# The second half's factors made row-wise and transposed by the DMA on load: a two-branch kernel on one core

## The chip, the core and the metric

The kernel runs on one core of a Trainium2 chip. The metric is device time in microseconds, as the median of several executions. Five engines work side by side, each on its own queue of instructions in order: PE (TensorE, matrix products), DVE (VectorE), ACT (ScalarE), POOL (GpSimd) and SP (SyncE, which issues most transfers here). Sixteen DMA engines move the data; the profile gives their mean busy share. SBUF is the on-chip memory with 128 partitions, PSUM the memory into which PE writes, DRAM the large memory outside.

## What is computed

```
xn = layernorm(A_q)                                   # 2048 x 1024
conv(kv): kv = shiftconv(A_k) * A_v; y = longconv(kv, A_ssm_k) + kv * A_ssm_D
out = A_q + xn * y + silu(xn @ B_w1) @ B_w2            # B_w1 1024 x 3584, B_w2 3584 x 1024
```

The first branch is a causal convolution of length 2048 for each of 1024 channels. The second is a feed-forward block with 3584 hidden units. All inputs are 32-bit floats. Large products are made with 16-bit parts: each operand is split into a high and a low half-precision part, and three products (high x high, high x low, low x high) are added.

## The kernel before, in words

**The row tiles.** The 2048 rows are 16 tiles of 128 rows by 1024 columns. `load_row` loads each into a buffer `xt`, `ln_rows` normalizes it in place (line 501). PE needs the 1024 columns on partitions, so `transposes` (line 507) turns each 128 x 128 block on PE by a product with an identity (line 520), four blocks to one PSUM bank `ft`.

**The products.** The first large product is made by Strassen's scheme: each 2 x 2 block product takes seven products P1 to P7 in place of eight, with sums of blocks as operands. The operands on the side of x are A11, A12, A22, S1, S2, S3, S4 (`PRODUCTS`, line 39): with the upper tile's halves A11, A12 and the lower tile's halves A21, A22, S1 = A21 + A22, S2 = S1 - A11, S3 = A11 - A21, S4 = A12 - S2. Tiles 0 to 3 (upper) and 4 to 7 (lower) make the operands of the first half, tiles 8 to 11 and 12 to 15 those of the second. One operand of one half is a tile of 128 partitions by 4 row tiles by 4 column blocks by 2 parts by 128, 16-bit: 1024 KB, one of eight places `x0` to `x7` (`XPLACE`, line 41).

`units` (line 948) runs 12 units of the first half, then 14 of the second. A unit's products run in the order P7, P6, P2, P5, then P1 of the next unit, P3, P4; each is 12 matrix instructions 512 wide, lines 912 to 914 in turn, so four of line 912 mark one product. Weight factors stand in a pool `wo`. For units 0 and 1 of the second half they were kept there; those of units 2 to 13 are loaded back (`load_factors`, line 783, `wo<-ws`).

**The second half's operands.** The place of an operand comes free when the last unit of the first half has read it. So the second half's operands are made early, from about 125 to 200 us, and stored in DRAM. `lower_sums` (line 570) and `upper_sums` (line 585) take the transposed blocks from PSUM, make the sums in buffers of the rings `s`, `s1` and `xst`, and hand each operand to `spill` (line 643). That splits it into its two 16-bit parts (`split`, line 352: ACT writes the high part, line 342; DVE the low part, line 334; DVE's sums are line 331) and stores it in `xsp`. `load_x` (line 985) later loads each operand with one plain transfer of 1024 KB, as soon as its place is free and all 28 stores have landed.

**What sets the order.** The order is planned when the program is built. Each piece of work is an `Op` with an engine, a busy time and, for a transfer, its bytes. `Order.run` (line 165) takes, again and again, the stream whose next piece can start first by the model, less a bias that acts as a priority (0.02 for the spill work here, 0.06 for `load_x`). `L` (line 322) is the cost of a plain load or store issued by SP. What comes out is a fixed order for each engine and for SP's queue of transfers; at run time every instruction waits in that order for its semaphores.

The convolution starts when the operands of the second half are stored (`change`, line 1695); from then on its work on DVE and ACT, and its smaller products on PE (lines 1437, 1471 to 1473, 1664 to 1666), are woven between the units. Its loads, the stores of the hidden values (`hs`, `hsf`), and copies of x to the output (`out<-in_x`, line 1185) stand in the same SP queue.

`Ring` is a set of equal buffers, `Halves` a set of larger buffers that are given out whole or by halves. `quad` (line 795) makes the same four sums for the second large product, in place and with rows on partitions.

Of the kernel before, what the change touches and what calls it, by code (L numbers as in the profile page):

```python
# [13 lines left out]
F16 = mybir.dt.float16  # L14
# [4 lines left out]
ADD, SUB, MUL = ALU.add, ALU.subtract, ALU.mult  # L19

P = 128
# [6 lines left out]
KH = KD // 2  # L28
NF = F // P
NP = NF // 2  # L30
W = 512
# [4 lines left out]
XS = 512.0  # L36
# [69 lines left out]
class Order:  # L106
# [182 lines left out]
def h3_ffn_kernel(ctx, tc, x, kp, vs, fs, shift, dskip, w1, w2, cfwd, cinv, out):  # L289
    nc = tc.nc  # L290
    ctx.enter_context(tc.manual_schedule())
    order = Order()
    add = order.add
    flag = defaultdict(Token)
# [12 lines left out]
    def size(a):  # L307
        n = 1
        for s in a.shape[1:]:
            n *= s  # L310
        return n
# [10 lines left out]
    def L(o, i, m=0.3):  # L322
        n = size(o) * o.shape[0] * mybir.dt.size(o.dtype)
        return Op("SP", 0.4, 0.1, lambda: nc.sync.dma_start(o, i), [i], [o], m, n)

    def G(o, i, m=0.3):
        n = size(i) * i.shape[0] * mybir.dt.size(i.dtype)
        return Op("POOL", 1.1, 3.0, lambda: nc.gpsimd.dma_start(o, i, accum_op=ADD), [i], [o], m, n)  # L328

    def v_tt(o, a, b, op, **k):  # L330
        return V(lambda: nc.vector.tensor_tensor(o, a, b, op=op), o, [a, b], **k)  # L331
# [32 lines left out]
    xsp = {p[0]: dram.tile([P, 4, KH, 2, P], F16, name=f"xsp{p[0]}") for p in PRODUCTS.values()}  # L364
# [38 lines left out]
    lnp = early.enter_context(tc.tile_pool(name="lnp", bufs=1))  # L403
# [1 line left out]
    ft = Ring(order, ps_e, "ft", 3)  # L405
    nm = Ring(order, ps_e, "nm", 1)
    xts_r = Ring(order, lnp, "xt", 12)
    sums_r = Ring(order, lnp, "s", 4)
    s1_r = Ring(order, lnp, "s1", 4)
    xst_r = Ring(order, lnp, "xst", 3)  # L410
    raw_r = Ring(order, rawa, "raw", 4)
    t1_r = Ring(order, rawa, "t1", 1)
    sq_r = Ring(order, rawa, "ss", 2)
# [93 lines left out]
    def transposes():  # L507
        jobs = [(t, a) for t in range(4) for a in range(2)]
        jobs += [(4 + i, a) for i in range(4) for a in range(2)]
        for i in range(4):  # L510
            jobs += [(12 + i, 0), (12 + i, 1), (8 + i, 0), (8 + i, 1)]
        for t, a in jobs:
            yield flag["xn", t]
            xn, tok = xns[t]
            yield ft.ready
            pt, ptok = ft.tile([P, KH, P], uses=2)

            def mm():
                for c in range(KH):
                    nc.tensor.transpose(pt[:, c, :], xn[:, (KH * a + c) * P:(KH * a + c + 1) * P], ident)  # L520
            yield T(mm, pt, [xn], 0.5, m=0.3)
            tok.set()
            pts.append((pt, ptok))
# [34 lines left out]
    def next_transposed():  # L558
        yield next_pt
        return pts.pop(0)  # L560
# [9 lines left out]
    def lower_sums(to, ring):  # L570

        a21, k21 = yield from next_transposed()
        c21, kc = yield from next_sum(sums_r, 1)
        yield a_act(c21, a21, AF.Copy)
        k21.set()
        give(to, "A21", a21, k21)
        a22, k22 = yield from next_transposed()
        s1, ks1 = yield from next_sum(ring, 2)
        yield v_tt(s1, a22, c21, ADD)
        k22.set()  # L580
        give(to, "A22", a22, k22)
        give(to, "S1", s1, ks1)
        return c21, kc, s1, ks1

    def upper_sums(to, ring, c21, kc, s1, ks1, t=None):

        if t is not None:
            yield flag["kept", t]
        a11, k11 = kept[t][0] if t is not None else (yield from next_transposed())
# [8 lines left out]
        a12, k12 = kept[t][1] if t is not None else (yield from next_transposed())  # L598
# [9 lines left out]
    def x_rows():  # L608
        yield from first_rows()
        second["A21"], second["tok"] = places[4].tile([P, 4, KH, 2, P], F16)  # L610
        for name in ("A22", "S2", "S3", "S1", "S4"):
            r = places[XPLACE[name]]
            yield r.ready
            xo[0][name], xtok[0][name] = r.tile([P, 4, KH, 2, P], F16)

        class Kept:
            bias = 0.14

            def __init__(self, i):
# [17 lines left out]
        class Spilled(Kept):  # L637
            bias = 0.02

            def __call__(self, name):  # L640
                return None if name == "A21" else lambda src, tok: spill(xsp[name][:, self.i], src, tok)

        def spill(o, src, tok):
            yield lambda: s1_r.ready() or xst_r.ready()
            r = s1_r if s1_r.ready() else xst_r
            st, stok = r.tile([P, KH, 2, P], F16)
            yield from split(st[:, :, 0], st[:, :, 1], src, XS, (tok,))
            yield L(o, st)
            stok.set()
            flag["spilled"].set()  # L650

        yield 0.02
        for i in range(4):
            part = yield from lower_sums(Spilled(i), sums_r)
            yield from upper_sums(Spilled(i), sums_r, *part)
        flag["x done"].set()

    for name in ("A11", "A12", "A21", "A22", "S1", "S2", "S3", "S4"):
        flag["x", 0, name] = Token(4)
# [325 lines left out]
    def load_x():  # L985
        yield flag["spilled"]
        for name in [p[0] for p in PRODUCTS.values()]:
            r = places[XPLACE[name]]
            yield r.ready
            xo[1][name], xtok[1][name] = r.tile([P, 4, KH, 2, P], F16)  # L990
            yield L(xo[1][name], xsp[name])
            flag["x", 1, name].set()


# [802 lines left out]
```

## Time and profile before

| | |
|---|---|
| median of 3 executions | 1277.92 us (1276.17 to 1280.69) |
| the profiled execution | 1277.71 us |
| its span on the core | 1275.9 us |
| mean granted TensorE clock | 0.994 |
| DMA, all queues | 284.55 MB, mean 223 GB/s |
| issues of `x<-xsp` | 7 of 1024 KB |
| issues of `xsp<-s` and `xsp<-xst` | 28 of 256 KB |

The span is the stretch of time that the profile shows, from the first to the last instruction. A row of a group gives line, engine, operation, output and inputs by name, the shapes, the count, then busy time and mean duration, then the engine's idle time ahead of the group with what ended it. A row of the order of time begins with start and duration in microseconds. Rows by stage give the stretch, its length and each engine's busy time in it. A row of transfers gives name, queue, count, size and the median time from issue to landing. PE instructions overlap in a pipeline: one of 512 columns is shown as 0.38 us long, but the next starts 0.21 or 0.22 us after it.

### The profile page before, as it was taken

The numbers are of one execution on the slowest core, as the hardware profiler recorded it, in microseconds if no ns is written. First come the engines' busy times: TensorE is split into PE (matmuls) and PEld (weight loads), VectorE is DVE, ScalarE is ACT, GpSimd is POOL, SyncE is SP. The second block draws the span as 40 slices with busy tenths as digits, with TensorE's granted clock in tenths as the row PEclk, the third lists the DMA queues.
The fourth block names the chain that finished last, engine by engine and source line by source line (L and its number), as shares of the span: only waits on it lengthen the run. The fifth ranks groups of instructions, "written<-read, shape, count | busy, mean of one in ns | idle before, by whom it ended". The sixth has DMA issues, their size and how long they took to land.

```text
span 1275.9 us, 17270 instructions
## 1 busy us (share of the span) xinstructions
PE 1244.9 (98%) x6146; PEld 609.6 (48%) x6146; DVE 1148.4 (90%) x1533; ACT 729.5 (57%) x1169; POOL 132.9 (10%) x141
## 2 busy tenths in 40 slices
PE   7899999999999999999999999999999999999997
PEld 6444444444444544445444544544444454454453
DVE  8999997998899879999899799899979989998981
ACT  6867887878776777559651722653452263544231
POOL 0000000000000110002100300300020030123132
PEclk8999999999999999999999999999999999999999
DMA  9457799889998999569984774697395496778776
GB/s 330 157 161 226 270 321 316 289 257 345 337 363 283 305 295 339 155 199 304 309 251 114 166 202 109 147 284 218 92 223 150 108 201 204 220 149 144 159 130 88
DMA packets 220102, 284.55 MB, mean 223 GB/s; under 512 B 14960, under 2 KB 133744, under 8 KB 217840
## 3 DMA queue, kind: packets, MB, share of 16 engines
q1 hardware_dynamic: 193280, 258.54, 62.2%
q0 software_dynamic: 26736, 24.92, 15.2%
q8 instruction: 48, 0.79, 0.2%
q14 instruction: 38, 0.31, 0.1%
HBM read 193.22 MB, written 98.57 MB: 229 GB/s over the span
## 4 chain that ended last, share of the span: by engine, by line
PE 72%; DVE 11%; issue 8%; DMA 5%; ACT 3%; POOL 1%; SPq 0%; POOLq 0%; DVEq 0%; ACTq 0%
PE ff L912 12%; PE ff L913 12%; PE ff L914 12%; PE ff L1040 9%; PE ff L1041 9%; PE ff L1042 9%; DVE spec L331 3%; PE ps L1471 1%; PE ps L1473 1%; PE ps L1472 1%; DVE tmp L331 1%; DVE x L334 1%; DMA x<-in_w 1%; POOL out L328 1%; DMA out<-yt 1%
## 5 line engine op out<-in xcount | busy, mean ns | idle before, releaser
L1040 PE MATMUL ff<-x,wo 128*128 128x512 f16 x864 | 327.4, 379 | 4.5 <-ACT hf L342 4.1
L1042 PE MATMUL ff<-x,wo 128*128 128x512 f16 x864 | 327.4, 379 | 0.0
L1041 PE MATMUL ff<-x,wo 128*128 128x512 f16 x864 | 327.4, 379 | 0.0
L913 PE MATMUL ff<-x,wo 128*128 128x512 f16 (+1 forms) x808 | 303.9, 376 | 2.1 <-DVE x L334 2.1
L912 PE MATMUL ff<-x,wo 128*128 128x512 f16 (+1 forms) x808 | 303.9, 376 | 1.9 <-ACT hf L342 1.4
L914 PE MATMUL ff<-x,wo 128*128 128x512 f16 (+1 forms) x808 | 303.8, 376 | 0.3 <-DVE wo L334 0.3
L331 DVE TENSOR_TENSOR spec<-spec 128x512 f32<-128x512 f32 (+2 forms) x256 | 261.2, 1052 | 2.5
L1041 PEld LDWEIGHTS <-wo 128*128 128x128 f16 x864 | 84.5, 98 | 104.1 <-issue 5.7
L1042 PEld LDWEIGHTS <-wo 128*128 128x128 f16 x864 | 84.6, 98 | 101.9
L1040 PEld LDWEIGHTS <-wo 128*128 128x128 f16 x864 | 85.5, 99 | 98.8
L914 PEld LDWEIGHTS <-wo 128*128 128x128 f16 x808 | 79.3, 98 | 95.9 <-issue 3.1
L912 PEld LDWEIGHTS <-wo 128*128 128x128 f16 x808 | 80.8, 100 | 86.5 <-issue 0.7
L913 PEld LDWEIGHTS <-wo 128*128 128x128 f16 x808 | 79.3, 98 | 89.2 <-issue 3.0
L328 POOL DMA_DIRECT2D out<-yt x64 | 71.6, 1333 | 339.9 <-DVE yt L334 207.7
L328 POOL DMA_DIRECT2D out<-hf x63 | 56.2, 892 | 470.9 <-ACT hf L342 408.8
L342 ACT ACTIVATE hf<-ff,invc 128x512 f32<-128x512 f32 x64 | 43.4, 680 | 106.9 <-PE ff L1042 78.0
L331 DVE TENSOR_TENSOR tmp<-spec 128x2048 f32<-128x2048 f32 (+1 forms) x48 | 92.5, 1933 | 1.1
L342 ACT ACTIVATE spec<-spec 128x1024 bf16<-128x1024 f32 x32 | 33.8, 1055 | 83.0 <-DVE spec L331 82.8
L334 DVE SCALAR_TENSOR_TENSOR ht<-hf,wsc,ht 128x1024 f16<-128x1024 f32 (+1 forms) x56 | 67.3, 1201 | 6.7 <-ACT ht L342 6.7
L342 ACT ACTIVATE ht<-hf,wsc 128x1024 f16<-128x1024 f32 (+1 forms) x56 | 60.8, 1086 | 7.1 <-DVE hf L331 4.1
L334 DVE SCALAR_TENSOR_TENSOR acc<-kin,taps,acc 128x1024 f32<-128x1024 f32 x48 | 61.3, 1278 | 3.5 <-ACT acc L342 3.5
L342 ACT ACTIVATE zh<-spec,csc 128x1024 f16<-128x1024 f32 x31 | 35.0, 1143 | 47.9 <-DVE spec L334 46.4
(189 smaller groups left out, 1791.6 us busy)
## 6 DMA issues: line engine op xcount, KB each, us to landing
wo<-hs SPq DMA_DIRECT2D x160, 256.0 KB, 3.6
hs<-ht SPq DMA_DIRECT2D x80, 256.0 KB, 5.0
out<-hf POOLq DMA_DIRECT2D x63, 256.0 KB, 4.3
raw<-in_w SPq DMA_DIRECT2D x28, 512.0 KB, 5.7
wraw<-in_w SPq DMA_DIRECT2D x24, 512.0 KB, 5.9
w2n<-in_w SPq DMA_DIRECT2D x24, 512.0 KB, 6.5
kin<-in_kp SPq DMA_DIRECT2D x16, 704.0 KB, 4.8
xt<-in_x SPq DMA_DIRECT2D x16, 512.0 KB, 7.4
```

Source lines behind the costliest of these rows:

```text
L328: return Op("POOL", 1.1, 3.0, lambda: nc.gpsimd.dma_start(o, i, accum_op=ADD), [i], [o], m, n)
L331: return V(lambda: nc.vector.tensor_tensor(o, a, b, op=op), o, [a, b], **k)
L334: return V(lambda: nc.vector.scalar_tensor_tensor(o, a, s, b, op0=op0, op1=op1), o, [a, b] + ([] if isinstance(s, float) else [s]), **k)
L342: nc.scalar.activation(o, i, func, scale=scale, **kw)
L912: nc.tensor.matmul(o, w[:, 0, k], xf[:, :, k, 0], start=first and k == 0, stop=False, **kw)
L913: nc.tensor.matmul(o, w[:, 0, k], xf[:, :, k, 1], start=False, stop=False, **kw)
L914: nc.tensor.matmul(o, w[:, 1, k], xf[:, :, k, 0], start=False, stop=last and k == KH - 1, **kw)
L1040: nc.tensor.matmul(po, hx[:, n, 0, :], wc[:, n, 0, :], start=first and n == 0, stop=False, **kw)
L1041: nc.tensor.matmul(po, hx[:, n, 0, :], wc[:, n, 1, :], start=False, stop=False, **kw)
L1042: nc.tensor.matmul(po, hx[:, n, 1, :], wc[:, n, 0, :], start=False, stop=last and n == 3, **kw)
L1471: nc.tensor.matmul(ps, cf[:, 0], hi[:, i], start=i == 0, stop=False, **kw)
L1472: nc.tensor.matmul(ps, cf[:, 0], lo[:, i], start=False, stop=False, **kw)
```

## The change

For tiles 8 to 15 no transposes are made on PE. `more_sums` waits for both tiles of a pair to be normalized, splits and stores A11 and A12 (the upper tile whole) and A22 as they are, rows on partitions, then makes S1 over A22, S3 over A21, S2 over A11 and S4 over A12, in the tile's own buffer, and stores these in pairs. `load_x` then loads each operand by a transfer that transposes: partition and column are exchanged in every 128 x 128 block of 16-bit elements. The planner counts for it 0.6 us of SP and 1.2 times the bytes. The three rings of 4, 4 and 3 buffers of 2 KB a partition become one `Halves` of six 4 KB buffers. The first half's operands are made as before.

```
+    def X(o, i, m=0.3):
+        n = size(o) * o.shape[0] * mybir.dt.size(o.dtype)
+        return Op("SP", 0.6, 0.1, lambda: nc.sync.dma_start(o, i, transpose=True), [i], [o], m, 1.2 * n)
...
-    sums_r = Ring(order, lnp, "s", 4)
-    s1_r = Ring(order, lnp, "s1", 4)
-    xst_r = Ring(order, lnp, "xst", 3)
+    sums_r = s1_r = xst_r = Halves(order, lnp, "s", 6)
...
         jobs += [(4 + i, a) for i in range(4) for a in range(2)]
-        for i in range(4):
-            jobs += [(12 + i, 0), (12 + i, 1), (8 + i, 0), (8 + i, 1)]
...
         for i in range(4):
-            part = yield from lower_sums(Spilled(i), sums_r)
-            yield from upper_sums(Spilled(i), sums_r, *part)
+            yield from more_sums(i)
         flag["x done"].set()
+    def more_sums(i):
+        def spill(names, src, tok):
+            yield xst_r.ready if len(names) == 1 else xst_r.pairs
+            rows, rtok = place(names)
+            yield from split(rows[:, :, 0], rows[:, :, 1], src.rearrange("p (k w) -> p k w", w=P), XS, (tok,))
+            for n, name in enumerate(names):
+                yield L(xsp[name][:, i], rows[:, n * KH:(n + 1) * KH])
+                flag["spilled"].set()
+            rtok.set()
+        def place(names):
+            return (xst_r.tile if len(names) == 1 else xst_r.pair)([P, len(names) * KH, 2, P], F16)
+        yield flag["xn", 8 + i]
+        yield flag["xn", 12 + i]
+        (up, utok), (low, ltok) = xns[8 + i], xns[12 + i]
+        x, y, z, v = up[:, 0:W], up[:, W:], low[:, 0:W], low[:, W:]
+        none = Token()
+        yield from spill(("A11", "A12"), up, none)
+        yield from spill(("A22",), v, none)
+        yield v_tt(v, z, v, ADD)
+        yield v_tt(z, x, z, SUB)
+        add(spill(("S3", "S1"), low, ltok), 0.02)
+        yield v_tt(x, v, x, SUB)
+        ltok.set()
+        yield v_tt(y, y, x, SUB)
+        utok.set()
+        add(spill(("S2", "S4"), up, utok), 0.02)
...
-            yield L(xo[1][name], xsp[name])
+            yield X(xo[1][name].rearrange("p i k h w -> p (i k h) w"), xsp[name].rearrange("p i k h w -> p (i k h w)"))
```

More of the change, by code (lines that the diff above doesn't have):

```diff
@@ L583, in lower_sums, with upper_sums @@
         return c21, kc, s1, ks1
[L585 to L589, printed above, removed]
+    def upper_sums(to, ring, c21, kc, s1, ks1, t):
+        yield flag["kept", t]
+        a11, k11 = kept[t][0]
         s2, ks2 = yield from next_sum(ring, 2)
@@ L597, in upper_sums @@
         give(to, "S3", c21, kc)
-        a12, k12 = kept[t][1] if t is not None else (yield from next_transposed())
+        a12, k12 = kept[t][1]
         s4, ks4 = yield from next_sum(ring, 1)
@@ L635, in x_rows @@
             yield from upper_sums(Kept(i), xst_r, *half[i], t=i)
[L637 to L650, printed above, removed]
         yield 0.02
         for i in range(4):
-            part = yield from lower_sums(Spilled(i), sums_r)
-            yield from upper_sums(Spilled(i), sums_r, *part)
+            yield from more_sums(i)
         flag["x done"].set()
+    def more_sums(i):
[24 more added lines that the diff above has]
+        add(spill(("S2", "S4"), up, utok), 0.02)
     for name in ("A11", "A12", "A21", "A22", "S1", "S2", "S3", "S4"):
```

## The prediction

> **What bounds the kernel now.** I read the page's totals and its 40 slices first, then busy times by stage, then the groups of TensorE instructions, and last the order of time around the two places that the diff touches.
>
> ```profile
> span 1275.9 us, 17270 instructions
> PE 1244.9 (98%) x6146; PEld 609.6 (48%) x6146; DVE 1148.4 (90%) x1533; ACT 729.5 (57%) x1169; POOL 132.9 (10%) x141
> PE   7899999999999999999999999999999999999997
> DMA  9457799889998999569984774697395496778776
> ```
>
> The span is 1275.9 us, and the profiled execution took 1277.71 us, 0.2 us below the median of 1277.92; 1.8 us lie around the span. PE is busy all the way except at both ends, so a PE slot that is freed in the middle is time gained, if nobody else takes it back. DMA is in its eighth to tenth tenths from slice 7 to 13. The busy times by stage (PE, PEld, DVE, ACT, POOL, granted clock, DMA share, GB/s) narrow that down:
>
> ```profile
> 125.00:200.00 75.00, 74.22 (x370) 36.47 (x368) 73.19 (x123) 63.78 (x98) 0.00 (x0) 1.00 0.86 295
> 200.00:280.00 80.00, 80.00 (x380) 37.05 (x378) 68.61 (x107) 61.99 (x89) 0.95 (x1) 1.00 0.87 289
> 280.00:330.00 50.00, 50.00 (x241) 23.75 (x240) 43.33 (x58) 39.78 (x59) 0.76 (x1) 1.00 0.96 315
> 330.00:400.00 70.00, 70.00 (x332) 32.44 (x330) 66.38 (x70) 49.31 (x81) 0.00 (x0) 1.00 0.99 342
> ```
>
> Two things are to be seen. From 125 to 200 us, where the last eight row tiles are transposed and their factors made, PE idles 0.8 us and VectorE 1.8 us: two engines are full. From 280 to 400 us, where the second half's factors come back, PE never idles and the DMA engines are 96 to 99% busy. So the change takes work from PE in a stage that PE bounds, and alters seven loads in a stage in which the DMA has no spare time.
>
> **The change part by part: the transposes removed.** The jobs for tiles 8 to 15 go: 8 tiles x 8 blocks, 64 of the 128 transposes of line 520, in 16 groups of four.
>
> ```profile
> L520 PE MATMUL ft<-ident,xt 128*128 128x128 f32 x128 | 19.8, 290 | 9.8 <-DVE x L334 3.5 <-DVE xt L501 3.1 <-ACT xt L342 2.1
> ```
>
> The 290 ns is a pipelined duration and isn't the price. The price is how far a group pushes the next product back, read from the starts in order of time:
>
> ```profile
> 138.42 0.63 PE L520 MATMUL ft<-ident,xt 128*128 128x128 f32 x4 [0.53 <-DVE s L334]
> ...
> 141.26 0.38 PE L914 MATMUL ff<-x,wo 128*128 128x512 f16 x1
> 141.48 0.60 PE L520 MATMUL ft<-ident,xt 128*128 128x128 f32 x4
> 141.91 0.38 PE L912 MATMUL ff<-x,wo 128*128 128x512 f16 x1
> ...
> 163.75 0.38 PE L914 MATMUL ff<-x,wo 128*128 128x512 f16 x1
> 163.97 0.63 PE L520 MATMUL ft<-ident,xt 128*128 128x128 f32 x4
> 164.44 0.38 PE L912 MATMUL ff<-x,wo 128*128 128x512 f16 x1
> ```
>
> Here a group takes 141.91 - 141.48 = 0.43 us, there 164.44 - 163.97 = 0.47 us; 16 x 0.45 = 7.2 us. The first of these groups also waited 0.53 us for VectorE to empty a bank; without transposes that wait goes too. What is late next is the product itself, whose operands were ready: PE ran it without a gap. Gain on PE: **7.7 us**.
>
> **Sums and splits.** Before, each of four pairs of tiles had one ScalarE copy, four VectorE sums and seven splits of 512 wide, one instruction per engine each. After, it has the same four sums, in place in SBUF, and three splits 1024 wide with one 512 wide; the copy goes.
>
> ```profile
> L334 DVE SCALAR_TENSOR_TENSOR s<-ft,s x9: 680/680/683, 137.6 to 198.4; 128x512 f16<-128x512 f32 x9
> L342 ACT ACTIVATE s<-ft x17: 573/577/599, 41.6 to 195.7; 128x512 f16<-128x512 f32 x9, 128x512 f32<-128x512 f32 x8
> 126.51 1.28 DVE L334 SCALAR_TENSOR_TENSOR wo<-raw,wsc,wo 128x1024 f16<-128x1024 f32 x1
> 129.15 1.13 ACT L342 ACTIVATE wo<-raw,wsc 128x1024 f16<-128x1024 f32 x1
> ```
>
> VectorE's splits fall from 7 x 0.68 = 4.8 to 3 x 1.28 + 0.68 = 4.5 us a pair, 1.0 us over four. ScalarE falls from 8 x 0.58 = 4.6 to 3 x 1.13 + 0.58 = 4.0 us, 2.6 us over four. I take nothing for either: PE covers both engines. Without that cover VectorE would limit the stage, which is the second rival. The in-place sums add waits: S1 is written over A22, so it waits for both halves of A22's split; S2 is written over A11, behind the split of the upper tile. What is queued behind them on VectorE is the weight splits, for which PE waits. I price the waits at nothing because the planner's order places a sum only when its model says that the split is over, and because other streams fill between; the other end is one 1.28 us split for each pair, 5 us. The stores to DRAM stay 28 of 256 KB with 2 KB rows, so SP issues as many as before. The three rings of 4 + 4 + 3 buffers become twelve halves; for the first eight tiles I take nothing.
>
> **The seven loads.** SP issues seven loads of 1024 KB, each behind the last product that reads its place: the first at 282.10, the last (A22) at 313.63. From 301.99 each product has four instructions of L912: P1, the upper half's last P3 and P4, then P7, P6, P2, P5, P1, P3 and, at 332.21, the P4 that reads A22.
>
> ```profile
> 282.10 0.33 SPq L324 DMA_DIRECT2D x<-xspA  x1
> 313.63 0.32 SPq L324 DMA_DIRECT2D x<-xspA  x1
> 345.71 1.39 SPq L324 DMA_DIRECT2D wo<-ws_B  x1
> ```
>
> ```profile
> 301.99 0.38 PE L912 MATMUL ff<-x,wo 128*128 128x512 f16 x1
> 332.21 0.38 PE L912 MATMUL ff<-x,wo 128*128 128x512 f16 x1
> 363.94 0.38 PE L912 MATMUL ff<-x,wo 128*128 128x512 f16 x1
> ```
>
> ```profile
> x<-xspS SPq DMA_DIRECT2D x4, 1024.0 KB, 7.2
> x<-xspA SPq DMA_DIRECT2D x3, 1024.0 KB, 5.9
> wo<-ws_B SPq DMA_DIRECT2D x12, 256.0 KB, 6.3
> out<-hf SPq DMA_DIRECT2D x1, 256.0 KB, 2.0
> ```
>
> A11 has 301.99 - 282.10 = 19.9 us to its use, of which 5.9 go to landing. A22 has 18.6, less 5.9: 12.7 us in hand. The weight load behind them that is tightest, B11 of the fourth lower unit, has 363.94 - 345.71 = 18.2, less 6.3: **11.9 us** in hand. Since the DMA engines are full, every microsecond that a load grows is carried to all that follow, and what exceeds 11.9 us in sum stands on PE.
>
> How much a load grows no row of before shows; I bound it by packets. Two windows with different mixes, 95 to 110 us and 340 to 345 us:
>
> ```profile
> DMA packets 3940, 4.10 MB, mean 273 GB/s; under 512 B 192, under 2 KB 3264, under 8 KB 3938
> q1 hardware_dynamic: 3938, 4.07, 83.3%
> ```
>
> ```profile
> DMA packets 963, 1.83 MB, mean 365 GB/s; under 512 B 72, under 2 KB 72, under 8 KB 963
> q1 hardware_dynamic: 963, 1.83, 103.6%
> ```
>
> The first: 0.833 x 16 x 15 us over 3938 packets is 50.8 ns at a mean of 1033 B. The second: 1.036 x 16 x 5 us over 963 is 86.1 ns at 1900 B. The line through them has 8.7 ns a packet and 0.0407 ns a byte. A plain load of 1 MiB at the second window's 365 GB/s takes 2.9 us of all 16 engines: the lower end, since the same bytes move. Transposed, the longest piece with one destination pattern is a row of one 128 x 128 block, 256 B: 19.2 ns by the line, and 4096 / 16 x 19.2 = **4.9 us**. If it goes in pieces of 16 elements (32 B, 10.0 ns), it is 32768 / 16 x 10.0 = 20.5 us, the upper end. I take 4.9, because 256 B rows are how the source lies and because it is nearest to the rows measured.
>
> Growth: 7 x (4.9 - 2.9) = 14.0 us, less 11.9 in hand: 2.1 us on PE. **The sum**: 1277.7 - 7.7 + 2.1 = 1272.1, and with the 0.2 to the median 1272.3 us. In general the time is 1270.2 + max(0, 7 x (T - 2.9) - 11.9) for a load of T us. The gain is all gone at T = 5.7; 0.3% (3.8 us) faster needs T below 5.1, and 3.8 us slower needs T above 6.2. 0.3% is about what a measurement of this kernel can tell from no change.
>
> The Trainium skill, on the page "DMA: Bandwidth & Descriptors", section "Latency and other measured facts", gives 261 GB/s for a DMA transpose with a non-contiguous middle dimension and 350 to 400 for a contiguous one. By the lower of these, as an estimate, a load takes 4.0 us, all growth is hidden, and the sum would be 1270.2 us; no run here shows it yet.
>
> **The rivals.**
>
> *The freed PE time is not passed on* (0.22). For: VectorE has 1.8 us idle from 125 to 200, and with its own 1.0 us the stage can shrink by 2.8 us only; in-place sums hold the same queue. Against: the spill work has the lowest priority and can move past 200 us, where VectorE idles 11.4 us before 280. Price: 7.7 becomes 2.8 us, less 2.1: 1277.2 us. A load of 5.1 to 6.2 us ends in the same place.
>
> *The transposed loads outlast their lead* (0.31; the one on the slower side). Place: P3 and P4 of the first lower units and the weight loads behind them; it decides from T = 5.7. For: the DMA row at 0.96 to 0.99, and SP, which serves everything in order, so that spills, signal loads and weights all stand behind a long load, and the engines that wait for those behind them. Against: the 4.9 us. Price at the geometric middle of the ends, 7.7 us: 7 x 4.8 - 11.9 = 21.7, so 1291.9 us; at 20.5 us it would be 1381.
>
> *The blocks go one after another, each with its own round trip* (0.05). The quickest landing above is 2.0 us; 32 blocks make 64 us a load: 7 x 61.1 - 11.9 = 416, so 1686 us. Against: no load of before shows such a chain, and 16 engines share each. The Trainium skill speaks for it on the page "VectorE: DVE Perf Modes", section "The three transpose paths", with 1309 ns for one 128 x 128 block by DMA; 32 in a row would be an estimated 42 us a load, and some 1530 us in all.
>
> **How the numbers follow.** The forecast, 1272.3 us, has 0.42: its loads take up to 5.1 us. By the formula its own range is 1270 to 1274, and 1268 if waits beside the transposes go too. Faster by over 0.3%: 0.41, all of it the forecast. Within 0.3%: 0.22 from the first rival and 0.01 from the forecast's edge, 0.23. Slower: 0.31 + 0.05 = 0.36. The range goes from 1268 to 1292: it leaves out the serial blocks (0.05), about 0.13 of the outlasting loads (T over 7.7) and 0.02 below.
>
> **What would show it.** Line 520 has 64 transposes, none after 100 us, and products run unbroken from 125 to 200. The seven loads land in 8 to 11 us instead of 5.9 to 7.2; the first idle PE, if any, stands ahead of the first lower unit's P3 or P4 and is ended by a DMA into x. If PE is idle there for over 8 us, the second rival holds. If VectorE shows no idle time from 125 to 200 while PE waits for wo, the first does. The forecast is wrong, too, if the planner, whose costs for these steps are new, orders the later stages otherwise: PE's idle time from 400 us on would then change without any of the steps above.

## The result and the profile after

The changed kernel takes 1280.84 us (median of 17 executions, 1279.70 to 1284.61), the kernel before 1277.80 us beside it (17 executions, 1275.46 to 1280.69). The ratio is 1.0029, with a 95% interval of 1.0022 to 1.0036: slower by 3 us, where 5.6 us faster was forecast. The profiled execution took 1281.56 us, its span is 1279.8 us. Lines 324, 331, 334, 342, 520 and 912 to 914 of the kernel before are lines 324, 336, 339, 347, 521 and 926 to 928 now; the transposing load is line 329.

The page of the kernel after, totals, slices of PE and of DMA, and the packets; then the packets of the kernel before:

```profile
PE 1244.7 (97%) x6082; PEld 604.2 (47%) x6082; DVE 1146.4 (90%) x1521; ACT 725.5 (57%) x1153; POOL 133.0 (10%) x141
PE   7899999989899999999999999999999999999997
DMA  9447899889999899669995684598486487877766
DMA packets 247988, 284.53 MB, mean 222 GB/s; under 512 B 43744, under 2 KB 162528, under 8 KB 246624
```

```profile
DMA packets 220102, 284.55 MB, mean 223 GB/s; under 512 B 14960, under 2 KB 133744, under 8 KB 217840
```

PE has exactly 64 matrix instructions fewer, and 0.2 us less busy time, so the saving was eaten within "busy" as well as beside it. Two slices of PE, the ninth and the eleventh, are no longer full. The packets under 512 B rise by 28784; 7 x 4096 = 28672 of them are 256 B rows of the seven loads.

By stage (PE, PEld, DVE, ACT, POOL, granted clock, DMA share, GB/s), the kernel after:

```profile
125.00:200.00 75.00, 75.00 (x355) 34.64 (x353) 73.77 (x112) 63.13 (x85) 0.00 (x0) 1.00 0.90 304
200.00:280.00 80.00, 75.05 (x346) 33.74 (x344) 66.60 (x100) 57.74 (x84) 0.95 (x1) 0.98 0.82 272
280.00:330.00 50.00, 46.74 (x210) 21.34 (x209) 39.55 (x60) 35.48 (x51) 0.00 (x0) 0.94 1.03 244
330.00:400.00 70.00, 66.69 (x309) 30.32 (x308) 62.85 (x68) 44.59 (x75) 0.76 (x1) 0.99 1.04 347
```

From 125 to 200 us the change did what it was to do: PE is full, and 355 instructions are left of 370 although 48 transposes have gone from this stretch (the other 16 stood at 119.7 to 122.3 us), which means that 33 products moved up. From 200 to 400 us, where PE had been busy without a gap, it idles 4.95 + 3.26 + 3.31 us, and its clock is not full in any of the three stretches. The GB/s from 280 to 330 fall from 315 to 244 while the DMA engines' share rises from 0.96 to 1.03.

The groups that answer to the prediction's steps: transposes, transposing loads on SP (the three numbers are the shortest, median and longest time in ns that the instruction held SP), and their issue to landing.

```profile
L521 PE MATMUL ft<-ident,xt x64: 272/273/329, 10.4 to 50.9; 128*128 128x128 f32 x64
```

```profile
L329 SPq DMA_TRANSPOSE x<-xspS x4: 4546/6285/6567, 292.9 to 321.7; - x4
L329 SPq DMA_TRANSPOSE x<-xspA x3: 4697/5480/5812, 283.0 to 329.1; - x3
```

```profile
x<-xspS SPq DMA_TRANSPOSE x4, 8.4
x<-xspA SPq DMA_TRANSPOSE x3, 8.1
```

The transposes, line 521 now, are 64 and none comes after 51 us; the loads land in 8.1 and 8.4 us, as foreseen. What was not foreseen is the middle pair: a plain load held SP for 0.33 us, a transposing one holds it for **4.5 to 6.6 us**. SP's order of time shows what that does to the transfers behind it, VectorE's when the values to be stored were ready, ScalarE's what comes of it, and PE's what that costs:

```profile
302.13 6.57 SPq L329 DMA_TRANSPOSE x<-xspS  x1
308.79 1.08 SPq L324 DMA_DIRECT2D hsfS<-ht  x2
309.97 5.81 SPq L329 DMA_TRANSPOSE x<-xspA  x1
315.88 4.55 SPq L329 DMA_TRANSPOSE x<-xspS  x1
320.52 1.08 SPq L324 DMA_DIRECT2D hsfS<-ht  x2
```

```profile
314.53 1.28 DVE L339 SCALAR_TENSOR_TENSOR ht<-x,wsc,ht 128x1024 f16<-128x1024 f32 x1
```

```profile
324.64 0.72 ACT L347 ACTIVATE ht<-hf,wsc 128x512 f16<-128x512 f32 x1 [4.74 <-DMA hsfS<-ht]
...
326.83 0.59 ACT L347 ACTIVATE hf<-ff 128x512 f32<-128x512 f32 x1
```

```profile
324.21 0.38 PE L928 MATMUL ff<-x,wo 128*128 128x512 f16 x1
327.48 0.52 PE L926 MATMUL ff<-x,wo 128*128 128x512 f16 x1 [2.89 <-ACT hf L347]
327.79 0.63 PE L927 MATMUL ff<-x,wo 128*128 128x512 f16 x1
328.22 0.63 PE L928 MATMUL ff<-x,wo 128*128 128x512 f16 x1
```

Read it backwards. PE stands at 324.6 until ScalarE has emptied a bank (`hf<-ff`, 326.83). ScalarE had stood 4.74 us because it needed a buffer `ht`, which is free only when its store to `hsfS` has landed. That store was issued at 320.52, though its values were ready at 315.81 (`ht<-x`), because SP was held from 309.97 to 320.43 by two loads in a row. The starts of PE after the stall are 0.43 us apart (327.79, 328.22), where they were 0.216 before it: the stall costs more than its 2.89 us. ScalarE's waits from 283 to 360 us, in the kernel after and in the one before (line, what it waited for, total, times, longest):

```profile
ACT ht L347 <- DMA hsfA<-ht: 9.3, 3, 3.5
ACT ht L347 <- DMA hsfS<-ht: 7.1, 4, 4.7
```

```profile
ACT ht L342 <- DMA hsfA<-ht: 0.9, 1, 0.9
ACT ht L342 <- DMA hsfS<-ht: 0.7, 1, 0.7
```

They rise from 1.6 to 16.4 us. An idle PE ended by a DMA into `x`, which the prediction named as the first sign of trouble, doesn't occur. There is one earlier stall, at 273 us, ahead of all seven loads:

```profile
273.09 0.38 PE L928 MATMUL ff<-x,wo 128*128 128x512 f16 x1
276.37 0.61 PE L926 MATMUL ff<-x,wo 128*128 128x512 f16 x1 [2.90 <-ACT wo L347]
```

It is the place of the first rival: weight splits that come late, with VectorE busy 9.8 to 10.0 of every 10 us from 240 to 280. So two theories stand. **H** (hold): SP's queue, held by each transposing load, delays the stores and with them ScalarE and PE. **V** (VectorE): the freed PE time ran into the engines that make the weights, at 273 us, and what follows is a consequence.

### The profile page after: what moved, and what is told of

Read it like the earlier page. It is cut to its first block, busy times and chain, and to the rows that moved or that the text cites. A ratio compares the mean times of both kernels' runs of the same rounds, so it can differ in the third digit from the quotient of the medians.

```text
span 1279.8 us, 17054 instructions
## 1 busy us (share of the span) xinstructions
PE 1244.7 (97%) x6082; PEld 604.2 (47%) x6082; DVE 1146.4 (90%) x1521; ACT 725.5 (57%) x1153; POOL 133.0 (10%) x141
## 5 line engine op out<-in xcount | busy, mean ns | idle before, releaser
L333 POOL DMA_DIRECT2D out<-yt x64 | 74.5, 1362 | 338.5 <-DVE yt L339 220.9
L347 ACT ACTIVATE ht<-hf,wsc 128x1024 f16<-128x1024 f32 (+1 forms) x56 | 60.5, 1083 | 11.4 <-DMA hsfS<-ht 6.9
L339 DVE SCALAR_TENSOR_TENSOR wo<-raw,wsc,wo 128x512 f16<-128x512 f32 (+1 forms) x56 | 56.1, 1012 | 9.0 <-ACT wo L347 9.0
```

The lines of the kernel that those rows point to most:

```text
L339: return V(lambda: nc.vector.scalar_tensor_tensor(o, a, s, b, op0=op0, op1=op1), o, [a, b] + ([] if isinstance(s, float) else [s]), **k)
L347: nc.scalar.activation(o, i, func, scale=scale, **kw)
```

## The experiments

Medians are given with the ratio to the kernel before on the same chip and its 95% interval. The stage that tells most is 283 to 360 us, whose row counts the PE instructions that were done in it; a product instruction takes 0.216 us. The kernel before took 1277.2 to 1278.1 us in these comparisons. The runs e1, e6 and e15 to e18 keep each engine's planned order as in the kernel after; in all others the edit changes what the planner counts, and with it the order.

**e1_plain_load.** The seven operands are loaded as they lie, without transposing; all else, each engine's order too, is that of the kernel after.

```
-        lambda: nc.sync.dma_start(o, i, transpose=True)
+        lambda: nc.sync.dma_start(o, i)
...
-            yield X(xo[1][name].rearrange(...), xsp[name].rearrange(...))
+            yield X(xo[1][name], xsp[name])
```

> The changed kernel with the same planned order on every engine; only the seven loads are plain instead of transposing, so the second half's operands arrive untransposed (that part of the result is left wrong). Queue theory (each transposing load holds SP for 4.5 to 6.6 us, stores of hidden values wait behind it, ScalarE waits for their buffers, PE for ScalarE): SP holds of 0.3 to 0.8 us, PE loss between 283 and 360 us falls from about 10 us to under 2, the loss at 270 to 283 us stays near 7; the time falls to 1270 to 1276 us. VectorE theory (all of the lost gain is VectorE without slack before 283 us): the time stays within 2 us of 1281.

Measured: 1271.26 us, 0.9955 (0.9942 to 0.9967). The rows of 283 to 360 us, of the kernel before, the kernel after and e1:

```profile
283.00:360.00 77.00, 77.00 (x364) 35.75 (x363) 67.52 (x79) 60.99 (x94) 0.76 (x1) 1.00 1.01 341
```

```profile
283.00:360.00 77.00, 71.87 (x328) 32.71 (x327) 60.43 (x72) 50.48 (x76) 0.76 (x1) 0.98 1.03 273
```

```profile
283.00:360.00 77.00, 76.53 (x363) 35.70 (x362) 69.74 (x82) 59.33 (x92) 0.76 (x1) 1.00 0.99 339
```

e1 does 363 PE instructions there, the kernel after 328: 35 x 0.216 = 7.6 us of the 9.6 us between them. ScalarE doesn't wait for a store of hidden values there in e1. So the removal of the transposes and the new order of the stores are worth 1277.41 - 1271.26 = 6.1 us, and the transposing loads cost 1280.84 - 1271.26 = 9.6 us. The stall at 273 us is in e1 too (2.90 us, at 271.8), which speaks against V already. The plain loads land in 7.3 and 8.3 us there, nearly as late as the transposing ones, so the landing says little about transposing.

**e2_before_transposing.** The kernel before, its PE transposes kept, with the seven loads as transposing ones (so its operands are turned twice). The planner counts them as in the kernel after, and its order changes with that.

```
-            yield L(xo[1][name], xsp[name])
+            yield X(xo[1][name].rearrange(...), xsp[name].rearrange(...))
```

> The kernel before with one change: its seven loads are transposing ones with the planner's cost of the changed kernel (what they load was transposed already, so that part of the result is left wrong). PE still makes all 128 transposes. If the loads cost the same wherever they stand, it is 9.6 us (the changed kernel less e1_plain_load) above before: 1286 to 1289. If the loads only hurt because PE arrives early at a VectorE that is behind, it stays under 1281.

Measured: 1292.04 us, 1.0107 (1.0090 to 1.0125). The loads and the order that comes with them cost 14.5 us, more than in the kernel after and above the forecast. ScalarE waits 15.1 us for the stores from 283 to 360 us, and there is no stall at 273 us. So a kernel can be slow in the way of H without the stall of V.

**e6_plain_256.** As e1, but each load with an access pattern of 256 B pieces, as a transposing load reads. The trace counts 1024 packets of 1 KB for such a load, where a transposing one has 4096 of 256 B.

```
+            yield X(xo[1][name].rearrange("p i k h w -> p (i k h) w"),
+                    xsp[name].rearrange("p i k h w -> (p i k h) w").rearrange("(n p) w -> p n w", p=P))
```

> As e1_plain_load, with the same planned order, but each plain load moves its 1024 KB in 4096 rows of 256 B, as the transposing load does, so the DMA engines have the work of the transposing loads (18 ns a packet, 4.6 us a load) while nothing is transposed (that part of the result is left wrong). SP theory (what costs is that SP is held while a transposing load is fed): SP held under 1.5 us a load, time within 2 us of e1_plain_load's 1271.3. Packet theory (what costs is the DMA engines' longer work in a full stage): time 1278 to 1282, near the changed kernel's.

Measured: 1276.52 us (11 executions), 0.9992 (0.9983 to 1.0002), 5.3 us over e1 and between the two forecasts. SP's order of time shows where the queue is held then:

```profile
319.64 0.98 SPq L329 DMA_DIRECT2D x<-xspS  x1
320.72 5.60 SPq L324 DMA_DIRECT2D hsfA<-ht  x2
```

The load itself is off SP in 0.68 to 0.98 us, but the transfer behind it, whatever it is, then holds SP for 3.7 to 6.4 us (a pair of stores takes 1.08 us in the kernel after). The queue is held without any transposition. Adding, for the seven loads, the time from the start of a load's issue to the end of the next transfer's issue (waits for buffers included) gives 13.8 us in the kernel before, 15.7 in e1, 43.1 in e6 and 48.9 in the kernel after. And the DMA engines while nearly nothing but such loads runs, in the kernel after (318.5 to 320.5 us), in e6 and, with plain loads, in e1 (317 to 320 us):

```profile
DMA packets 2254, 0.58 MB, mean 289 GB/s; under 512 B 2254, under 2 KB 2254, under 8 KB 2254
q1 hardware_dynamic: 2254, 0.58, 127.3%
```

```profile
DMA packets 642, 0.65 MB, mean 217 GB/s; under 512 B 1, under 2 KB 642, under 8 KB 642
q1 hardware_dynamic: 642, 0.65, 113.9%
```

```profile
DMA packets 157, 1.16 MB, mean 385 GB/s; under 512 B 16, under 2 KB 16, under 8 KB 16
```

A row of a transposing load takes 1.273 x 16 x 2 us / 2254 = 18.1 ns of packet time, and 4096 / 16 x 18.1 = 4.6 us a load. But a share above 100% means that packets overlap: at the 289 GB/s that were moved, a load takes 3.6 us. The load of e6, at 217 GB/s, takes 4.8 us, a plain one at 385 GB/s 2.7 us. So e6 loads the DMA engines for longer than the transposing loads do, and is still the faster kernel.

**e17_hold and e18_hold_256.** The hold without the transposition: e1 (e18: e6), with a 64 KB store of a part of the loaded operand to a scratch tensor behind each load. SP has to wait for the landing before it can issue that store.

```
-        lambda: nc.sync.dma_start(o, i)
+        lambda: (nc.sync.dma_start(o, i), nc.sync.dma_start(scr, o[:, 3, 3]))
```

> e1_plain_load with the same planned order, and behind each plain load a store of 64 KB (512 bytes a partition) from the loaded tile, for which SP waits until the load has landed: SP held some 5 to 7 us a load, 0.45 MB more traffic, no transposition and no small rows (the operands arrive untransposed, so that part of the result is left wrong). If the hold costs by itself: 1275 to 1281 us. If not: within 2 us of e1_plain_load's 1271.3.

> e6_plain_256 with the same 64 KB store behind each load: rows of 256 bytes and SP held until each load has landed (7 to 9 us), no transposition (that part of the result is left wrong). If rows and hold make up the cost of a transposing load: 1281 us or, since the hold is longer here, up to 1288. If the transposition itself costs: within 2 us of e6_plain_256's 1276.5.

Measured: e17 1283.53 us, 1.0041 (1.0028 to 1.0053); e18 1297.04 us, 1.0147 (1.0131 to 1.0162). e17 has plain loads of 8 KB packets, which land sooner than those of the kernel before (5.4 and 6.0 us), and still it is 12.3 us over e1. SP, ScalarE, the waits and the stage in e17:

```profile
310.89 0.55 SPq L329 DMA_DIRECT2D x<-xspA  x1
316.56 0.33 SPq L329 DMA_DIRECT2D scr<-x  x1
316.99 0.38 SPq L329 DMA_DIRECT2D x<-xspS  x1
322.36 0.32 SPq L329 DMA_DIRECT2D scr<-x  x1
322.73 1.31 SPq L324 DMA_DIRECT2D hsfS<-ht  x2
```

```profile
325.54 0.72 ACT L347 ACTIVATE ht<-hf,wsc 128x512 f16<-128x512 f32 x1 [5.07 <-DMA hsfS<-ht]
```

```profile
283.00:360.00 77.00, 71.23 (x322) 32.31 (x321) 59.30 (x71) 50.54 (x76) 0.76 (x1) 0.96 0.81 270
```

The same store is late at the same place (322.73 against 320.52) and lets ScalarE stand as long (5.07 against 4.74), with the DMA engines at 0.81 and not at 1.03. By the sum used above, taken to the next transfer other than the probe's store, SP is held 47.3 us in e17, against 48.9 in the kernel after. A held queue is enough; busier DMA engines aren't needed. With the loads of e6 (e18) the sum is 60.5 us, and the time 25.8 us over e1. Both came out above the forecasts that allowed for a hold. The probe adds 0.46 MB of stores, whose own cost no run shows.

**e15_hold and e16_hold_256**, the same with a store of 2 B for each partition, failed as probes.

```
+        lambda: (nc.sync.dma_start(o, i), nc.sync.dma_start(scr, o[:, 0, 0, 0, 0:1]))
```

> e1_plain_load with the same planned order, and behind each plain load a store of 256 bytes from the loaded tile, for which SP must wait until the load has landed: SP is held some 5 to 8 us a load, with no transposition and no small rows (the operands arrive untransposed, so that part of the result is left wrong). If the hold costs by itself, 1274 to 1279 us; if not, within 1.5 us of e1_plain_load's 1271.3.

> e6_plain_256 with the same store behind each load: rows of 256 bytes and SP held until the load has landed, no transposition (that part of the result is left wrong). If rows and hold together make up the cost, the time comes to the changed kernel's 1281 or, since the hold is longer here, up to 1286. If the transposition itself costs, it stays within 1.5 us of e6_plain_256's 1276.5.

Measured: 1397.15 us, 1.0933 (1.0916 to 1.0951), and 1410.42 us, 1.1036 (1.1020 to 1.1052). In e15 the store took 18.2 us to land, and the loads behind such stores 22: a cost of the probe, which says nothing on the question.

**e4_stores_pool.** The kernel after; the stores of the first half's hidden values go through GpSimd's queue.

```
+    def PS(o, i, m=0.3):
+        return Op("POOL", 1.1, 0.1, lambda: nc.gpsimd.dma_start(o, i), [i], [o], m, n)
...
-                yield L(hsf[sp][name]...
+                yield (L if sp else PS)(hsf[sp][name]...
```

> The stores of the first half's hidden factors (hsf) are issued by GpSimd's queue in place of SP's, so they don't stand behind the transposing loads. Queue theory: ScalarE no longer waits for these stores between 283 and 360 us, PE loss there under 4 us instead of 10, time 1272 to 1278 us. Rival (growth of DMA work): no change there, 1280 to 1283 us.

Measured: 1283.62 us, 1.0048 (1.0036 to 1.0061). The longest wait of ScalarE from 283 to 360 us:

```profile
ACT wraw L351 <- DMA wraw<-in_w: 6.1, 1, 6.1
```

ScalarE's waits for those stores are nearly gone (1.4 us of 16.4), as H has it, but another transfer of SP's queue takes their place, and PE has a stall of 4.2 us behind it, until 344.98. In this plan another victim was found.

**e8_more_pool.** So the loads and copies that stood behind, too, go to GpSimd's queue: e4 with the first loads of the second weights, the loads of the second channel group (signals, filters, values) and the copies of x.

```
-                yield L(raw, w2r[...])
+                yield PS(raw, w2r[...])
...
-            yield L(kin, kp[g, b])
+            yield (PS if g == 1 else L)(kin, kp[g, b])
...
```

> The changed kernel with more of SP's queue moved to GpSimd's queue: the first half's hsf stores, the first loads of the second weight matrix, the copies of x to the output and the signal loads of channel group 1. SP keeps the operands, the weights and the rest. SP theory: waits behind transposing loads on ScalarE and VectorE between 283 and 360 us mostly go, PE loss there falls from 10 to under 5 us, time 1272 to 1279. Packet theory: the DMA engines have the same work, loss as before, 1280 to 1286.

Measured: 1296.26 us, 1.0146 (1.0117 to 1.0175). The largest wait of PE:

```profile
PE ff L930 <- DMA x<-xspS: 10.4, 2, 6.5
```

Now the prediction's second rival does appear in its own form, PE waiting for the operands, and SP is held 16.2 us by two of them in a row and 13.6 us by another. That the transfers on the other queue compete with the loads is the likely reason; no run shows it.

**e9_conv_later and e10_plain_later.** V: the convolution's start, and with it what fills VectorE at 240 to 280 us, is put off by 25 us, in the kernel after (e9) and in e1 (e10).

```
-        convolution(max(order.free["DVE"], order.free["ACT"]))
+        convolution(max(order.free["DVE"], order.free["ACT"]) + 25.0)
```

> The changed kernel with the convolution allowed to start 25 us later in the plan. If the stall at 273 us comes from the convolution's first sums standing ahead of weight splits in VectorE's queue, the PE loss from 240 to 290 us falls from 8.5 to under 4 us; if VectorE has too much work whatever the order, it stays. The later stages then decide the time: 1274 to 1284 us.

> e1_plain_load (plain loads, so that part of the result is left wrong) with the convolution's start 25 us later in the plan, as in e9_conv_later. If the stall at 273 us in the changed kernel costs time in the end, its 7 us go and the time is 1264 to 1268 us. If PE would only lose them elsewhere, because VectorE's total work sets the pace, it stays at 1269 to 1276.

Measured: e9 1287.38 us, 1.0086 (1.0071 to 1.0102); e10 1274.69 us (12 executions), 0.9971 (0.9961 to 0.9981). 240 to 290 us in the kernel after, in e1 and in e10:

```profile
240.00:290.00 50.00, 45.10 (x198) 19.81 (x197) 46.08 (x67) 36.44 (x52) 0.00 (x0) 0.93 0.80 247
```

```profile
240.00:290.00 50.00, 44.67 (x202) 19.95 (x201) 46.90 (x69) 37.83 (x55) 0.00 (x0) 0.97 0.85 267
```

```profile
240.00:290.00 50.00, 50.00 (x235) 22.82 (x234) 47.69 (x63) 40.25 (x57) 0.20 (x1) 1.00 0.97 319
```

The edit does what it is to do, PE has 235 instructions there and no gap (e10), and neither kernel gets faster. In e9 PE then comes early to the seven loads and waits for them (`x<-xspA` 4.4 us, `x<-xspS` 1.8 us). In e10 the time is lost again later: 19 instructions from 283 to 360 us (344 against 363), and from 400 to 1200 us the two kernels with plain loads do

```profile
400.00:1200.00 800.00, 798.07 (x3930) 386.54 (x3928) 738.18 (x866) 407.75 (x678) 110.44 (x112) 1.00 0.76 206
```

```profile
400.00:1200.00 800.00, 789.32 (x3886) 381.90 (x3884) 734.55 (x861) 402.36 (x667) 108.72 (x110) 1.00 0.74 200
```

3930 PE instructions (e1) against 3886 (e10). Taking the stall away gains nothing in this plan. Whether PE would have lost that time later in any case, or loses it because the convolution starts late, isn't separated. V falls as the cause of the result: e1 has the same stall and is 9.6 us faster than the kernel after.

**e11_fillers_later and e12_both_later.** The transfers and squares that fill the stage, the copies of x by three units and the squares until unit 2, are put off (e11), and e9's edit is added (e12).

```
-            yield flag["unit", a // 2]
+            yield flag["unit", a // 2 + 3]
...
         yield lambda: "wraw" in ctxs
+        yield flag["unit", 2]
```

> The changed kernel, but the copies of x to the output start three units later and the squares of the second weight matrix two units of the second half later, so that the stage with the transposing loads has less DMA work and fewer transfers in SP's queue. If the loss from 283 to 360 us is the loads against that filler work, it falls from 10 to under 6 us and the time is 1274 to 1279. If the stores and loads that PE's own units need are enough to cause it, it stays within 2 us of 1281.

> e11_fillers_later with the convolution's start 25 us later as well. If the two losses of the changed kernel are separate and both can be planned away, 1266 to 1273 us; if PE, coming earlier, then waits for the transposing loads themselves as in e9_conv_later, 1278 to 1286.

Measured: e11 1280.46 us (12 executions), 1.0021 (1.0009 to 1.0032), no difference from the kernel after; e12 1284.00 us, 1.0046 (1.0028 to 1.0063). Of e12 only the time is used here.

**e5_sums_pool.** V from the other side: the 16 in-place sums go from VectorE to GpSimd.

```
+    def p_tt(o, a, b, op):
+        return Op("POOL", 1.3, 0.2, lambda: nc.gpsimd.tensor_tensor(o, a, b, op=op), [a, b], [o], 0.15)
...
-        yield v_tt(v, z, v, ADD)
+        yield p_tt(v, z, v, ADD)
```

> The sixteen in-place sums of the last eight row tiles (16 x 0.69 = 11 us) go from VectorE to GpSimd. VectorE theory: the PE stall at 273 us and the clock lost after it go, PE loss between 240 and 290 us falls from 8.5 to under 3 us, time 1274 to 1279 us. Rival (the stall is caused by where the plan puts the convolution's first sums in VectorE's queue, not by how much work there is): the loss between 240 and 290 us stays above 5 us, time 1279 to 1283.

Measured: 1291.46 us, 1.0110 (1.0095 to 1.0126). The 273 us stall goes, but new ones stand between 145 and 205 us, and the waits for the stores stay. A test of V it is only in part, for the sums are slow there (last section).

**e3_pieces.** Each load in four transposing pieces, so that another transfer can get between.

```
+            for q in range(4):
+                yield X(xo[1][name][:, q].rearrange(...), xsp[name][:, q].rearrange(...))
```

> Each transposing load is cut into four of 256 KB, one row tile each, which other work may come between in SP's order. The DMA engines' work is the same. Queue theory: SP is held about 1.3 us a piece, stores get through sooner, PE loss between 283 and 360 us falls by half or more, time 1272 to 1278 us. Rival (the growth of DMA work in a full stage, wherever SP stands): the same loss, 1280 to 1283 us.

Measured: 1291.35 us, 1.0114 (1.0098 to 1.0130). Each piece holds SP for 1.3 to 3.1 us, but the planned order put another transfer between the pieces of two of the seven loads only, and ScalarE still waits 16.4 us for stores. Inconclusive as a test of H.

**e7_plan_hold.** The planner is told of the hold: 5.6 us of SP, and 1.6 times the bytes.

```
-        return Op("SP", 0.6, 0.1, ..., [i], [o], m, 1.2 * n)
+        return Op("SP", 5.6, 0.1, ..., [i], [o], m, 1.6 * n)
```

> The changed kernel, but the planner is told what the trace showed of a transposing load: SP held for 5.6 us in place of 0.6, and 1.6 times the bytes in place of 1.2. If the loss from 283 to 360 us comes from a plan that doesn't know of the hold, SP's order changes and the loss there falls from 10 to under 5 us, time 1273 to 1278 us. If SP's capacity itself is short, no order helps: 1279 to 1285 us.

Measured: 1286.95 us, 1.0076 (1.0061 to 1.0090). A planner that knows of the hold finds no better order in this scheme. ScalarE's waits for the stores from 283 to 360 us fall from 16.4 to 4.6 us, but PE does 315 instructions there, fewer than in the kernel after (328): it now waits 6.8 us for weight splits and 1.7 us for a weight load. None of the four runs that were to relieve the queue (e3, e4, e7, e8) came into the time that H had put down for it; H rests on e1 and e17.

**e13_half and e14_quarter.** Two of the four pairs of tiles (e14: one) are made row-wise and loaded by transposing transfers, the others by PE as before.

```
+            if i < 2:
+                yield from more_sums(i)
+                continue
+            part = yield from lower_sums(Spilled(i), sums_r)
...
+            yield X(xo[1][name][:, 0:2].rearrange(...), xsp[name][:, 0:2].rearrange(...))
+            yield L(xo[1][name][:, 2:], xsp[name][:, 2:])
```

> The kernel before with half of the change: the first two of the four tile pairs are made row-wise and transposed by the DMA (half of each load, 512 KB), the other two by PE and loaded plainly. 32 PE transposes fewer, worth 3.1 us by half of e1_plain_load's gain. If the cost of transposing loads sets in past a point (what other work has in hand), it is under 2 us and the time is 1274 to 1276.5. If it goes with the bytes (half of 9.6), 1278 to 1281.

> A quarter of the change: one of the four tile pairs is made row-wise and transposed by the DMA. 16 PE transposes fewer, worth 1.5 us. Cost past a point: near none, 1275.5 to 1277. Cost in proportion to the bytes: 2.4 us, 1277.5 to 1279.5.

Measured: e13 1288.48 us, 1.0083 (1.0068 to 1.0098); e14 1278.96 us (12 executions), 1.0007 (0.9996 to 1.0018). Neither gains. In e13 each of the seven transposing halves still holds SP for 2.2 to 6.7 us, and PE waits 5.1 us for operands. Counted against half and a quarter of e1's gain, as the expectations did, the loads cost 13.6 us in e13 and 2.5 in e14, where all of the change costs 9.6: the quarter is as forecast for a cost in proportion to the bytes (2.4), the half lies above both forecasts. Each operand now comes in two transfers, and the order is another, so these kernels differ in more than the amount.

## Why the prediction was wrong, step by step

- **The transposes removed: right, and about its size.** The stage is full as foreseen, the 16 groups are gone, and with plain loads the kernel gains 6.1 us (e1) of the 7.7 counted. (The row at 138.42 was not the first of these groups, as the prediction has it: four of the 16 stand at 119.66 to 122.26, at 0.44 us each, so the sum holds.) Sums and splits at nothing: no run shows a cost for them from 125 to 200 us; the in-place waits leave PE at 75.00 of 75.
- **The first rival, VectorE.** Its stall exists, later than thought (273 us), and costs 235 - 202 = 33 PE instructions, 7.1 us, from 240 to 290 us (e10 against e1). But edits that take it away gain nothing (e9, e10), and e1 has it and still gains 6.1 us, where this rival had left 2.8.
- **A load's time on the DMA engines: counted too long.** 4.9 us was forecast. That is about the packets' own time, 4.6 us, but packets overlap: with the engines full, a load took 3.6 us, and a plain one 2.7 where 2.9 was counted. The growth is 7 x 0.9 = 6.3 us, not 14.0, and lies within the 11.9 us in hand; by the prediction's formula that would be 1270.2 us. The Trainium skill's 261 GB/s (page "DMA: Bandwidth & Descriptors", section "Latency and other measured facts"), by which a load would take an estimated 4.0 us, is nearer than 4.9; its 350 to 400 for a contiguous case isn't reached, the trace has 289. The 1309 ns that the Trainium skill gives for one block (page "VectorE: DVE Perf Modes", section "The three transpose paths") don't carry over to 32 blocks in one transfer: each of the seven loads landed within 10.1 us, and the third rival is out.
- **The step that failed: "what exceeds 11.9 us in sum stands on PE", +2.1 us.** In its place stand 9.6 us, and by another path. The forecast's own path cost nothing: in the kernel after, PE never waits for an operand or for a weight load from 283 to 420 us. The cost went by SP. I had written of the second rival that "SP, which serves everything in order" would keep transfers behind a long load, but the sum has no term for the time for which a load's issue holds SP (0.33 us in the rows of before, 4.5 to 6.6 after), and the lead of what stands behind it was taken from weights with 11.9 us in hand. The stores of the hidden values stand there too, and with two pairs of buffers in turn they have hardly any lead: ScalarE's waits for them rise from 1.6 to 16.4 us. e17 shows the hold to be enough by itself; e1, which has neither the hold nor short rows nor the transposition, loses nothing in this stage (363 instructions against 364 before).
- **The second rival** had the sign and, in its words on SP's order, the reason. The rest of it didn't hold: it needed loads of 5.7 us or more, and PE waiting for operands, its own form, is not in the kernel after; it is seen where PE came earlier or the transfers were moved or cut (e8, e9, e13).
- **The range.** The measured 1280.84 us lies inside 1268 to 1292, but that is luck: the upper part of the range stood for loads that take longer on the DMA engines, and those took less time than forecast.
- **How large a stall becomes.** Several stalls of about 3 us are followed by starts at half pace, and then cost more than their length. The granted clock from 283 to 360 us is 1.00 in e6, whose longest PE wait there is 1.2 us, 0.98 in the kernel after (2.9 us) and 0.96 in e17 (3.4 us), as their times are ordered: 1276.5, 1280.8, 1283.5. That this is the reason for the order of the times is argued, not shown.

**What stays open.** e6 holds SP nearly as long as the kernel after (43 against 49 us over seven loads) and is 4.3 us faster. Whether that is the longer hold, the place where it falls (on the load or on the transfer behind it), the four times as many packets or the transposition, no run separates. Nor does the cost follow the length of the hold: e17, with 47 us, is slower than the kernel after. Why SP is held at all isn't visible in the trace; rows of the load issued at 315.88 still pass until about 321.9 us, 1.5 us after its hold has ended.

## What to carry to other kernels

When a transfer is changed, look at three times, not at one: the DMA engines', the landing's, and how long its issue holds the queue, with the transfers that stand behind it in the same queue. The lead to compare with is that of the follower with the least in hand, here a store whose buffer an engine wants back, not that of the transfer's own reader. And a new wait in the trace need not be what costs the time: check by an experiment that takes it away before blaming it.

## What the runs showed of the hardware that was not expected

- A load of 1 MiB in rows of 256 B holds SP's queue 4.5 to 6.6 us when it transposes; one without transposition, in packets of 1 KB (e6), holds the next transfer's issue 3.7 to 6.4 us instead. A plain load holds it for 0.33 us.
- PE's pace halved after idle stretches of 2.9 us, though not always at once. From 270 to 290 us in the kernel after (the third column from the end is the granted clock):

```profile
270.00:280.00 10.00, 6.40 (x25) 2.47 (x23) 9.90 (x14) 5.08 (x8) 0.00 (x0) 0.82 0.75 215
280.00:290.00 10.00, 10.00 (x42) 4.46 (x41) 6.46 (x14) 6.74 (x9) 0.00 (x0) 0.84 0.94 259
```

  From 280 to 290 us PE is busy all the time and does 42 instructions, where 10 / 0.216 would be 46; the starts are 0.43 us apart until 283.17. The Trainium skill, on the page "TensorE: Matmul & The Clock Gate", section "Part 1: The HAM clock gate (the "warmup" mystery)", gives 426.7 and 215.7 ns for a cold and a warm array with 512 columns, and a window of about 3.4 us: the trace agrees with the two paces, and shows the drop after 2.9 us already. The length of a wait alone doesn't decide: in e1 two products start 0.22 us apart behind a wait of 2.90 us (until 275.08), and the half pace comes at 276.81, after 1.13 us more of waiting.
- A store of 2 B for each of 128 partitions took 18.2 us from issue to landing (e15), where 64 KB in runs of 512 B took 1.5 (e17).
- GpSimd's sum of 128 x 512 values took 1.7 to 1.8 us on average (e5), against 0.69 us on VectorE, and VectorE's splits beside it took up to 2.3 us instead of 1.28.
